# Output evictions of a second matrix product: eleven buffers of whole rows and one accumulating DMA per token tile

## The chip, the cores and the metric

The kernel runs on one core of one Trainium2 chip. The metric is the device time of one execution in microseconds (us), as the median over several runs. Differences under about half a per cent are not told apart from no change.

## What is computed

Three layers follow each other: a linear attention with a normalised output, a layer of three gates whose maximum is taken, and a mixture of four experts. Only the last is touched here:

```python
def _moe2_ref(x, domain_probs, w1, w2):
    N, D = x.shape              # 2304 tokens, 512 columns
    E = w1.shape[0]             # 4 experts, 1024 hidden columns each
    p = domain_probs / (domain_probs.sum(-1, keepdims=True) + 1e-09)
    out = np.zeros((N, D), dtype=np.float32)
    for e in range(E):
        h = np.maximum(x @ w1[e], 0.0)
        out += p[:, e:e + 1] * (h @ w2[e])
    return out.astype(np.float32)
```

## The kernel before

Every product of float32 matrices is written as three products of a rounded high part and a low rest (hi times hi, lo times hi, hi times lo), and the products of two-by-two blocks go by Strassen's scheme (in Winograd's form), with seven block products where the plain way has eight.

The layer of the experts is a sequence of 24 **visits** (`visits`, L1104). A visit is one pair (q, sb): q, from 0 to 7, is a half of an expert's hidden columns, and sb, from 0 to 2, is a super-block of 768 tokens, in two blocks (blk) of three token tiles (i) of 128 tokens. Through even q the super-blocks go 0, 1, 2, through odd q 2, 1, 0, so that two visits of three change the super-block. A visit has two halves, r = 0 and 1, and a half has seven steps k. In each step TensorE does one block product of the first matrix (`product`, L594, through `seven`, L604: 6 matmuls of 384 columns). ScalarE then brings the result out of PSUM (`after_product`, L650; the copies stand at L658), and VectorE adds it up. Between these steps stand, in portions of `AFTER = (10, 9, 9, 8, 10, 9, 8)`, the 126 matmuls (L855, 256 columns each) of the **second product of the visit before** (`second`, L842). So each visit has 84 + 126 = 210 matmuls.

The second product has seven block products j = 0 to 6, 18 matmuls each, in two parts: token tiles i = 0 and 1 (half 0), then i = 2 (half 1). When a part is done, `after_second` (L818) evicts it. For j = 0 a copy within PSUM does it (L826). For the others ScalarE (L836, j = 1, 2, 3, 6) writes an eviction buffer, scaled by the token's weight p, or VectorE (L838, j = 4, 5) adds to what stands in it. Which j belongs to which block of tokens and to which half b of the 512 output columns, in the kernel before:

| j | engine | blk, b | buffer | then sent |
|---|---|---|---|---|
| 1 | ScalarE | 1, 1 | new | no |
| 2 | ScalarE | 0, 0 | new | yes |
| 3 | ScalarE | 0, 1 | new | no |
| 4 | VectorE | 0, 1 | that of j = 3 | yes |
| 5 | VectorE | 1, 1 | that of j = 1 | yes |
| 6 | ScalarE | 1, 0 | new | yes |

There are three buffers (`new_ev`, L798), each of three pieces of 256 columns, one per token tile: one in `fa`, two in the tile `late["w2"]` (`w2s` in the profile). `put_out` (L806) sends a piece of 128 tokens x 256 columns to the output with a DMA of GpSimd's queue: as a plain store for q = 0 (L814), with addition in memory for the others (L812). Two token tiles of the eighteen are put together from two batches and need two DMAs of 64 rows each.

The order of the work is written out by hand, and each engine takes its instructions in that order. Behind the evictions on ScalarE stand the copies of L658, on which the next `product` on TensorE depends, since it writes the same PSUM bank. GpSimd also makes the sums of the weights (`w1_sums`, L530, `w2_sums`, L558). SyncE's queue loads the operands of the next super-block, 768 KB per step k, in the second half of a visit that ends with a change of super-block (`op_load`, L1118), and the weights.

Of the kernel before, what the change touches and what calls it, by code (L numbers as in the profile page):

```python
# [13 lines left out]
ALU = mybir.AluOpType  # L14
# [7 lines left out]
def tile_attn_moe_moe2(  # L22
# [23 lines left out]
    nc = tc.nc  # L46
    B, H, S, D = q.shape
    NT, DM = out.shape
    FF = w1.shape[1]
    E, _, EF = e_w1.shape  # L50
    P = 128
# [46 lines left out]
    fa = cst.tile([P, NB * KT + 2 * T], F32, name="fa")  # L98
# [4 lines left out]
    def part(t, at, n, c=None):  # L103
        ap = t[:, at : at + n]
        return ap if c is None else ap.rearrange("p (c f) -> p c f", c=c)
# [14 lines left out]
    for b0 in range(0, B, 2):  # L120
        for b, s0 in ((b0, 0), (b0, 256), (b0, None), (b0 + 1, 0), (b0 + 1, 256)):
# [3 lines left out]
            else:  # L125
                rows = out[b * S + s0 : b * S + s0 + 256, :].rearrange("(p r) d -> r p d", r=2)
# [327 lines left out]
    HK = 2 * T  # L454
# [18 lines left out]
    late = {}  # L473
# [321 lines left out]
    JACC = (0, 2, 1, 0, 2, 0, 0)  # L795
    ev_turn = [0]

    def new_ev():  # L798
        ev_turn[0] += 1
        n = ev_turn[0] % 3  # L800
        return part(fa, 12 * HK, HK) if n == 0 else late["w2"][:, (n - 1) * HK : n * HK]

    def piece(acc, i):
        return acc[i // 2][:, i % 2 * 2 * P : (i % 2 + 1) * 2 * P]

    def put_out(q, sb, blk, b, ev, i):  # L806
        t = (2 * sb + blk) * TPB + i
        n = P // len(tiles[t])
        for x, rows in enumerate(tiles[t]):
            dst, src = rows[:, b * 2 * P : (b + 1) * 2 * P], ev[x * n : (x + 1) * n, i * 2 * P : (i + 1) * 2 * P]  # L810
            if q:
                nc.gpsimd.dma_start(out=dst, in_=src, accum_op=ALU.add)  # L812
            else:
                nc.gpsimd.dma_start(out=dst, in_=src)  # L814

    held = {}

    def after_second(gi, q, sb, j, half):  # L818

        acc = [ACC[(gi + x) % 3] for x in range(3)]  # L820
        ps = acc[JACC[j]]
        e = q // 2
        its = (0, 1) if half == 0 else (2,)
        if j == 0:
            w = 4 * P if half == 0 else 2 * P
            nc.scalar.activation(out=acc[1][half][:, :w], in_=ps[half][:, :w], func=AF.Copy)  # L826
            return
        if half == 0 and j in (1, 2, 3, 6):
            held[j] = new_ev()
        ev = held[{4: 3, 5: 1}.get(j, j)]  # L830
        for i in its:
            blk = {1: 1, 2: 0, 3: 0, 4: 0, 5: 1, 6: 1}[j]
            pe = p_all[:, (2 * sb + blk) * TPB + i, e : e + 1]
            o = ev[:, i * 2 * P : (i + 1) * 2 * P]
            if j in (1, 2, 3, 6):
                nc.scalar.activation(out=o, in_=piece(ps, i), func=AF.Copy, scale=pe)  # L836
            else:
                nc.vector.scalar_tensor_tensor(out=o, in0=piece(ps, i), scalar=pe, in1=o, op0=ALU.mult, op1=ALU.add)  # L838
            if j in (2, 4, 5, 6):
                put_out(q, sb, blk, {2: 0, 4: 1, 5: 1, 6: 0}[j], ev, i)  # L840

    def second(gi, q, sb):  # L842

# [41 lines left out]
    with tc.manual_schedule():  # L885
# [75 lines left out]
        for st in steps:  # L961
            st, *en = st.split(".")
            kind = st[0]
            at = [int(st[1:])] if kind in "cds" else [int(x) for x in st[1:]]
            if kind in "cds":
                n = at[0]
# [28 lines left out]
            elif kind == "A":  # L995
                i, j, f = at
                moe1_a(i, j, f, xs[j], *en)
            elif kind == "H":
                j, f = at
# [133 lines left out]
        for q in range(1, Q):  # L1133
            e, pr, n = q // 2, q % 2 * 2, 6 * q
# [33 lines left out]
        for n in range(2 * len(visits)):  # L1168
# [10 lines left out]
            for k in range(7):  # L1179
                t = 7 * n + k  # L1180
                product(r, k)
                after_product(n, k)
                if gi == 0:
                    lag_at(7 * len(units) + t)
                    go(fill, FILL_18[1 + t])
                    if r == 0:
                        for i in SPLIT.get((0, k), ()):
                            y_split(i)
                for _ in range(AFTER[k] if gi else 0):
                    ended = next(rest, None)  # L1190
                    if ended:
                        after_second(*of, *ended)
                for step in todo.pop(t, ()):
                    step()
                if gi + 1 < len(visits):
                    turn_y(gi, r, k)
                for step in plan.pop(t, ()):
                    step()
# [5 lines left out]
        for ended in second(gi - 1, *visits[gi - 1]):  # L1204
            if ended:
                after_second(gi - 1, *visits[gi - 1], *ended)
# [33 lines left out]
```

## Time and profile before

| | |
|---|---|
| median of 3 runs | 1316.18 us (1314.63 to 1321.26) |
| profiled execution, its own time | 1327.1 us |
| span of the profile | 1325.3 us |
| busy in the span: TensorE, VectorE, ScalarE, GpSimd | 1125.6, 756.0, 599.0, 492.2 us |
| the layer of the experts in it (second products) | from 410.4 us to the end |

The profile is of one execution, 11 us above the median. Its span runs from the first instruction to the last. TensorE's matmuls overlap, so its busy time is no measure of its rate. The granted clock (1.00 is 2.4 GHz, 0.50 is 1.2 GHz) tells how fast a matmul can run.

### The profile page before, as it was taken

The numbers are of one execution on the slowest core, as the hardware profiler recorded it, in microseconds if no ns is written. First come the engines' busy times: TensorE is split into PE (matmuls) and PEld (weight loads), VectorE is DVE, ScalarE is ACT, GpSimd is POOL, SyncE is SP. The second block draws the span as 40 slices with busy tenths as digits, with TensorE's granted clock in tenths as the row PEclk, the third lists the DMA queues.
The fourth block names the chain that finished last, engine by engine and source line by source line (L and its number), as shares of the span: only waits on it lengthen the run. The fifth ranks groups of instructions, "written<-read, shape, count | busy, mean of one in ns | idle before, by whom it ended". The sixth has DMA issues, their size and how long they took to land.

```text
span 1325.3 us, 19611 instructions
## 1 busy us (share of the span) xinstructions
PE 1125.6 (85%) x7318; PEld 1097.8 (83%) x7318; DVE 756.0 (57%) x1298; ACT 599.0 (45%) x1269; POOL 492.2 (37%) x552
## 2 busy tenths in 40 slices
PE   7899999999978899797978769887877987797985
PEld 6789999999968899686978769787876987796885
DVE  3899866666677666355546435553644554455442
ACT  2542344344356555354455435454443454354443
POOL 1356434201132352344236334423533352344234
PEclk8999999999988899899989879988988988899988
DMA  9935544232176536657655685665578456758645
GB/s 247 300 100 181 191 171 134 95 126 82 60 298 221 219 111 222 197 80 207 180 106 118 154 238 80 189 151 134 82 201 242 71 114 148 212 80 211 192 56 67
DMA packets 128271, 207.63 MB, mean 157 GB/s; under 512 B 16304, under 2 KB 102832, under 8 KB 128176
## 3 DMA queue, kind: packets, MB, share of 16 engines
q1 hardware_dynamic: 88944, 168.29, 37.9%
q0 software_dynamic: 38528, 37.77, 20.8%
q8 instruction: 57, 0.93, 0.3%
q10 hardware_dynamic: 704, 0.33, 0.1%
q14 instruction: 38, 0.31, 0.1%
HBM read 136.35 MB, written 69.99 MB: 156 GB/s over the span
## 4 chain that ended last, share of the span: by engine, by line
issue 33%; POOL 18%; DMA 7%; PE 5%; ACT 1%; DVE 1%; POOLq 0%; ACTq 0%; DVEq 0%
POOL out_dram L812 12%; DMA out_dram<-w2s 4%; DMA out_dram<-fa 3%; PE bank L604 3%; POOL fa L558 3%; PE bank L855 2%; POOL w1s L530 2%; POOL out_dram L814 1%; DVE w2s L838 0%; ACT wr L633 0%; DVE wl L500 0%; ACT fa L836 0%; ACT w2s L836 0%; ACT wl L536 0%; ACT hr L633 0%
## 5 line engine op out<-in xcount | busy, mean ns | idle before, releaser
L604 PE MATMUL bank<-rb,wl 128*128 128x384 f32 x1032 | 235.3, 368 | 141.0 <-ACT bank L658 141.0
L604 PEld LDWEIGHTS bank<-rb,wl 128*128 128x128 f32 x1032 | 195.2, 209 | 148.4 <-ACT bank L658 147.1
L855 PE MATMUL bank<-wr 128*128 128x256 f32 x1683 | 273.1, 296 | 8.9 <-DVE w2s L838 8.1
L812 POOL DMA_DIRECT2D out_dram<-w2s x184 | 162.1, 1109 | 314.3 <-ACT w2s L836 155.9
L855 PEld LDWEIGHTS bank<-wr 128*128 128x128 f32 x1683 | 252.9, 204 | 11.2 <-DVE w2s L838 9.8
L658 ACT ACTIVATE fa<-bank 128x384 f32<-128x384 f32 x192 | 94.4, 492 | 211.0 <-PE bank L604 210.1
L604 PE MATMUL bank<-xr,wl 128*128 128x384 f32 x864 | 176.5, 339 | 6.2 <-DVE fa L645 4.5
L604 PEld LDWEIGHTS bank<-xr,wl 128*128 128x128 f32 x864 | 146.5, 190 | 7.5 <-DVE fa L645 5.3
L812 POOL DMA_DIRECT2D out_dram<-fa x96 | 84.5, 1101 | 167.2 <-ACT fa L836 87.3
L836 ACT ACTIVATE w2s<-bank,p_all 128x256 f32<-128x256 f32 x192 | 80.0, 475 | 134.9 <-DMA out_dram<-w2s 105.7
L530 POOL TENSOR_TENSOR w1s<-w1s 128x256 f32<-128x256 f32 x96 | 88.8, 944 | 111.5 <-DMA w1s<-w_da 48.7
L640 DVE TENSOR_TENSOR wr<-fa,wr 128x384 fp32r<-128x384 f32 x138 | 81.6, 592 | 57.2 <-ACT wr L633 57.2
L855 PE MATMUL bank<-wr,hr 128*128 128x256 f32 x567 | 94.4, 287 | 4.1 <-ACT bank L826 2.2
L855 PEld LDWEIGHTS bank<-wr,hr 128*128 128x128 f32 x567 | 83.7, 194 | 5.5 <-ACT bank L826 2.4
L633 ACT ACTIVATE wr<-fa 128x384 fp32r<-128x384 f32 x144 | 75.4, 525 | 11.3 <-DVE fa L648 6.9
L836 ACT ACTIVATE fa<-bank,p_all 128x256 f32<-128x256 f32 x96 | 40.1, 474 | 79.0 <-DMA out_dram<-fa 65.8
L638 DVE SCALAR_TENSOR_TENSOR wr<-fa,wr 128x384 fp32r<-128x384 f32 x49 | 30.1, 615 | 73.3 <-ACT wr L633 73.3
L855 PE MATMUL bank<-wr,xr 128*128 128x256 f32 x396 | 68.3, 282 | 1.5 <-DVE w2s L838 1.3
L645 DVE TENSOR_TENSOR fa<-bank,fa 128x384 f32<-128x384 f32 x96 | 53.0, 553 | 21.8 <-ACT fa L658 19.8
L604 PE MATMUL bank<-op,wl 128*128 128x384 f32 x288 | 60.4, 346 | 4.7 <-ACT fa L658 4.7
L855 PEld LDWEIGHTS bank<-wr,xr 128*128 128x128 f32 x396 | 58.5, 188 | 2.4 <-DVE w2s L838 1.9
L500 DVE TENSOR_TENSOR wl<-w1s,wl 128x768 fp32r<-128x768 f32 (+1 forms) x30 | 34.6, 1155 | 43.9 <-ACT wl L536 43.9
(196 smaller groups left out, 2011.9 us busy)
## 6 DMA issues: line engine op xcount, KB each, us to landing
rb<-op_d SPq DMA_DIRECT2D x42, 768.0 KB, 5.9
xr<-op_d SPq DMA_DIRECT2D x42, 768.0 KB, 7.6
out_dram<-w2s POOLq DMA_DIRECT2D x172, 128.0 KB, 3.9
out_dram<-fa POOLq DMA_DIRECT2D x84, 128.0 KB, 4.3
op<-op_d SPq DMA_DIRECT2D x14, 768.0 KB, 7.7
stage_a<-in_moe_w_dram SPq DMA_DIRECT2D x18, 512.0 KB, 4.0
w1s<-in_moe_w_dram SPq DMA_DIRECT2D x30, 256.0 KB, 4.5
fa<-in_moe_w_dram SPq DMA_DIRECT2D x28, 256.0 KB, 6.6
```

The lines of the kernel that those rows point to most:

```text
L500: nc.vector.tensor_tensor(out=lo, in0=src, in1=f32(hi), op=ALU.subtract)
L530: eng.tensor_tensor(out=st[o], in0=st[a], in1=st[b], op=ALU.subtract)
L558: nc.gpsimd.tensor_tensor(out=st[o], in0=st[a], in1=st[b], op=op)
L604: nc.tensor.matmul(out, w[wi][:, c * P : (c + 1) * P], y[yi][:, c, :], start=(i == 0 and k in begin), stop=(i == 5), skip_group_check=k no ...
L633: nc.scalar.activation(out=ops[key][0], in_=src, func=AF.Relu if relu else AF.Copy)
L638: nc.vector.scalar_tensor_tensor(out=lo, in0=src, scalar=0.0, in1=f32(hi), op0=ALU.max, op1=ALU.subtract)
L640: nc.vector.tensor_tensor(out=lo, in0=src, in1=f32(hi), op=ALU.subtract)
L645: todo.setdefault(t, []).append(lambda: fn(*args, **kw))
L658: nc.scalar.activation(out=out, in_=in_, func=func)
L812: nc.gpsimd.dma_start(out=dst, in_=src, accum_op=ALU.add)
L836: nc.scalar.activation(out=o, in_=piece(ps, i), func=AF.Copy, scale=pe)
L855: nc.tensor.matmul(piece(ps, i), h[hi][:, i * P : (i + 1) * P], w[wi], start=fresh, stop=last, skip_group_check=True,)
```

## The change

A buffer now holds one whole output row of 512 columns per token, for one token tile. Each visit takes six of them, three for blk 1 at j = 1 and three for blk 0 at j = 2, and all later evictions of the same tile go into the same buffer, at column 0 or 256. There are nine such places in q = 0 and eleven afterwards: four in `w2s`, four in the tile `late["ow"]` (`ob` in the profile), one in `fa`, and two more in `fa` from q = 1 on. A token tile is sent once per visit, at j = 4 (blk 0) or j = 6 (blk 1), by one DMA of 128 rows of 2 KB in place of two of 128 rows of 1 KB.

```diff
--- before.py
+++ after.py
@@ -795,23 +795,24 @@
     JACC = (0, 2, 1, 0, 2, 0, 0)
     ev_turn = [0]
 
-    def new_ev():
+    def new_ev(q):
+        fa_at = (12 * HK,) if q == 0 else (12 * HK, 16 * 2 * P, 18 * 2 * P)
+        places = [(late[x], n * DM) for n in range(4) for x in ("w2", "ow")] + [(fa, at) for at in fa_at]
         ev_turn[0] += 1
-        n = ev_turn[0] % 3
-        return part(fa, 12 * HK, HK) if n == 0 else late["w2"][:, (n - 1) * HK : n * HK]
+        return part(*places[ev_turn[0] % len(places)], DM)
 
     def piece(acc, i):
         return acc[i // 2][:, i % 2 * 2 * P : (i % 2 + 1) * 2 * P]
 
-    def put_out(q, sb, blk, b, ev, i):
+    def put_out(q, sb, blk, ev, i):
         t = (2 * sb + blk) * TPB + i
         n = P // len(tiles[t])
         for x, rows in enumerate(tiles[t]):
-            dst, src = rows[:, b * 2 * P : (b + 1) * 2 * P], ev[x * n : (x + 1) * n, i * 2 * P : (i + 1) * 2 * P]
+            src = ev[x * n : (x + 1) * n, :]
             if q:
-                nc.gpsimd.dma_start(out=dst, in_=src, accum_op=ALU.add)
+                nc.gpsimd.dma_start(out=rows, in_=src, accum_op=ALU.add)
             else:
-                nc.gpsimd.dma_start(out=dst, in_=src)
+                nc.gpsimd.dma_start(out=rows, in_=src)
 
     held = {}
 
@@ -820,24 +821,23 @@
         acc = [ACC[(gi + x) % 3] for x in range(3)]
         ps = acc[JACC[j]]
         e = q // 2
-        its = (0, 1) if half == 0 else (2,)
         if j == 0:
             w = 4 * P if half == 0 else 2 * P
             nc.scalar.activation(out=acc[1][half][:, :w], in_=ps[half][:, :w], func=AF.Copy)
             return
-        if half == 0 and j in (1, 2, 3, 6):
-            held[j] = new_ev()
-        ev = held[{4: 3, 5: 1}.get(j, j)]
-        for i in its:
-            blk = {1: 1, 2: 0, 3: 0, 4: 0, 5: 1, 6: 1}[j]
+        blk, b = {1: (1, 1), 2: (0, 0), 3: (0, 1), 4: (0, 1), 5: (1, 1), 6: (1, 0)}[j]
+        for i in (0, 1) if half == 0 else (2,):
+            if j in (1, 2):
+                held[blk, i] = new_ev(q)
+            ev = held[blk, i]
             pe = p_all[:, (2 * sb + blk) * TPB + i, e : e + 1]
-            o = ev[:, i * 2 * P : (i + 1) * 2 * P]
+            o = ev[:, b * 2 * P : (b + 1) * 2 * P]
             if j in (1, 2, 3, 6):
                 nc.scalar.activation(out=o, in_=piece(ps, i), func=AF.Copy, scale=pe)
             else:
                 nc.vector.scalar_tensor_tensor(out=o, in0=piece(ps, i), scalar=pe, in1=o, op0=ALU.mult, op1=ALU.add)
-            if j in (2, 4, 5, 6):
-                put_out(q, sb, blk, {2: 0, 4: 1, 5: 1, 6: 0}[j], ev, i)
+            if j in (4, 6):
+                put_out(q, sb, blk, ev, i)
 
     def second(gi, q, sb):
```

The order of the instructions on TensorE and SyncE is that of before. On ScalarE it is so too, with other buffers and other waits. The end of the visit that lies at 748 to 791 us in the profile stands on ScalarE as follows in the kernel before. L836 are the evictions of j = 6, the second L658 the copy on which TensorE's next product depends, and a DMASW is a wait for an output DMA:

```order
L658 ACTIVATE fa<-bank_73 128x384 [waits PE_49,Activation_49]
L633 ACTIVATE wr<-fa 128x384 [waits DVE_49]
L836 ACTIVATE w2s<-bank_66,p_all 128x256 [waits DMASW0_49,PE_49]
L836 ACTIVATE w2s<-bank_66,p_all 128x256 [waits DMASW1_49]
L836 ACTIVATE w2s<-bank_67,p_all 128x256 [waits DMASW2_49,PE_49]
L633 ACTIVATE wr<-fa 128x384 [waits DVE_49]
L658 ACTIVATE bank_72<-bank_73 128x384 [waits DVE_49,PE_49]
L633 ACTIVATE wl<-fa 128x384
L658 ACTIVATE fa<-bank_72 128x384 [waits PE_49]
```

and in the changed kernel:

```order
L658 ACTIVATE fa<-bank_73 128x384 [waits PE_49,Activation_49]
L633 ACTIVATE wr<-fa 128x384 [waits DVE_49]
L836 ACTIVATE w2s<-bank_66,p_all 128x256 [waits PE_49]
L836 ACTIVATE ob<-bank_66,p_all 128x256
L836 ACTIVATE w2s<-bank_67,p_all 128x256 [waits PE_49]
L633 ACTIVATE wr<-fa 128x384 [waits DVE_49]
L658 ACTIVATE bank_72<-bank_73 128x384 [waits DVE_49,PE_49]
L633 ACTIVATE wl<-fa 128x384
L658 ACTIVATE fa<-bank_72 128x384 [waits PE_49]
```

The evictions no longer wait for a DMA. Only the waits for TensorE are left.

GpSimd's queue at the start of q = 4 in the kernel before, behind the DMAs of j = 6: four sums for the first matrix's weights (`w1s`), the DMAs of j = 2, four sums for the second matrix's weights (in `fa`), and the first DMA of j = 4:

```order
L530 TENSOR_TENSOR w1s<-w1s 128x256 [waits DMAHW7_49,DMAHW0_49]
L530 TENSOR_TENSOR w1s<-w1s 128x256 [waits Pool_49]
L530 TENSOR_TENSOR w1s<-w1s 128x256
L530 TENSOR_TENSOR w1s<-w1s 128x256 [waits Pool_49]
L812 DMA out_dram<-w2s 128x256 [waits DMASW2_49,Activation_49]
L812 DMA out_dram<-w2s 128x256 [waits DMASW3_49,Activation_49]
L812 DMA out_dram<-w2s 128x256 [waits DMASW4_49,Activation_49]
L558 TENSOR_TENSOR fa<-fa 128x256 [waits DMAHW1_49]
L558 TENSOR_TENSOR fa<-fa 128x256 [waits DMAHW2_49,Pool_49]
L558 TENSOR_TENSOR fa<-fa 128x256
L558 TENSOR_TENSOR fa<-fa 128x256 [waits Pool_49]
L812 DMA out_dram<-w2s 128x256 [waits DMASW5_49,DVE_49]
```

and in the changed kernel, from the same sums to the first DMA of j = 4:

```order
L530 TENSOR_TENSOR w1s<-w1s 128x256 [waits DMAHW7_49,DMAHW0_49]
L530 TENSOR_TENSOR w1s<-w1s 128x256 [waits Pool_49]
L530 TENSOR_TENSOR w1s<-w1s 128x256
L530 TENSOR_TENSOR w1s<-w1s 128x256 [waits Pool_49]
L558 TENSOR_TENSOR fa<-fa 128x256 [waits DMAHW1_49]
L558 TENSOR_TENSOR fa<-fa 128x256 [waits DMAHW2_49,Pool_49]
L558 TENSOR_TENSOR fa<-fa 128x256
L558 TENSOR_TENSOR fa<-fa 128x256 [waits Pool_49]
L813 DMA out_dram<-w2s 128x512 [waits DMASW1_49,DVE_49,Activation_49]
```

The DMAs of j = 2, which wait for ScalarE, no longer stand between the two sets of sums.

## Rows read from the trace of the kernel before

**Rows 1.** Stretches (--windows): time; each engine's busy us (instructions); clock; DMA share; GB/s

```profile
core 0: us, PE busy (x) PEld busy (x) DVE busy (x) ACT busy (x) POOL busy (x), PEclk, DMA share, GB/s
674.04:707.61 33.57, 30.73 (x215) 30.33 (x214) 18.05 (x34) 17.89 (x41) 14.81 (x19) 1.00 0.45 73
825.49:868.91 43.42, 32.93 (x213) 32.32 (x212) 22.91 (x37) 20.19 (x45) 19.70 (x22) 0.90 0.68 169
868.91:910.46 41.55, 31.59 (x212) 31.18 (x211) 17.87 (x33) 16.95 (x40) 14.71 (x17) 0.91 0.73 197
910.46:945.44 34.98, 32.14 (x212) 31.73 (x211) 18.21 (x34) 17.90 (x41) 14.85 (x19) 0.94 0.44 71
512.61:1300.40 787.79, 643.13 (x4208) 633.35 (x4206) 386.86 (x696) 363.91 (x811) 314.74 (x362) 0.91 0.62 148
447.77:478.53 30.76, 30.01 (x212) 29.80 (x211) 20.69 (x36) 17.68 (x42) 13.95 (x21) 1.00 0.37 121
```

**Rows 2.** Waits from 512.61 to 1300.4 us: total us, times, longest us

```profile
PE bank L604 <- ACT bank L658: 134.6, 25, 10.3
ACT w2s L836 <- DMA out_dram<-w2s: 105.7, 41, 9.3
...
ACT fa L836 <- DMA out_dram<-fa: 54.8, 17, 8.5
```

**Rows 3.** Timeline of a visit's end: start us, us, engine line, [idle before <-releaser]

```profile
776.23 1.36 PE L855 MATMUL bank<-wr 128*128 128x256 f32 x10
780.20 0.86 POOL L812 DMA_DIRECT2D out_dram<-w2s  x1 [3.30 <-issue]
782.62 0.47 ACT L836 ACTIVATE w2s<-bank,p_all 128x256 f32<-128x256 f32 x1 [9.35 <-DMA out_dram<-w2s]
...
786.59 0.47 ACT L836 ACTIVATE w2s<-bank,p_all 128x256 f32<-128x256 f32 x1 [2.57 <-DMA out_dram<-w2s]
...
787.38 0.48 ACT L658 ACTIVATE bank<-bank 128x384 f32<-128x384 f32 x1
...
787.91 2.29 PE L604 MATMUL bank<-rb,wl 128*128 128x384 f32 x6 [10.32 <-ACT bank L658]
```

**Rows 4.** DMA queues (packets, MB, share) and output DMAs (landing us), 512.61 to 1300.4

```profile
q0 software_dynamic: 34991, 31.51, 31.5%
q1 hardware_dynamic: 32304, 84.16, 30.2%
...
out_dram<-w2s POOLq DMA_DIRECT2D x146, 128.0 KB, 4.1
```

**Rows 5.** Line L812, output DMAs: ns min/median/max on GpSimd; landing in us

```profile
L812 POOL DMA_DIRECT2D out_dram<-w2s x184: 812/906/1893, 521.7 to 1310.7; - x184
...
DMA to landing us min/median/max: 2.5/4.2/11.6
```

**Rows 6.** Line L1118, operand loads on SyncE's queue, and their landing in us

```profile
L1118 SPq DMA_DIRECT2D rb<-op_d x42: 319/319/345, 490.4 to 1243.8; - x42
...
DMA to landing us min/median/max: 4.1/7.1/8.5
```

**Rows 7.** Timeline in the middle of a visit in which q changes

```profile
837.79 1.88 DVE L500 TENSOR_TENSOR wl<-w1s,wl 128x1024 fp32r<-128x1024 f32 x1 [2.82 <-ACT wl L536]
837.86 5.39 POOL L558 TENSOR_TENSOR fa<-fa 128x256 f32<-128x256 f32 x4
...
839.59 1.07 DVE L640 TENSOR_TENSOR wr<-fa,wr 128x384 fp32r<-128x384 f32 x1
840.59 1.07 DVE L648 SCALAR_TENSOR_TENSOR fa<-fa 128x384 f32<-128x384 f32 x1
...
842.22 0.47 ACT L658 ACTIVATE bank<-bank 128x384 f32<-128x384 f32 x1 [4.05 <-DVE fa L645]
...
842.75 1.32 PE L604 MATMUL bank<-rb,wl 128*128 128x384 f32 x6 [2.83 <-ACT bank L658]
```

**Rows 8.** Timeline of VectorE in a visit without sums on GpSimd

```profile
676.00 0.55 DVE L640 TENSOR_TENSOR wr<-fa,wr 128x384 fp32r<-128x384 f32 x1
```

**Rows 9.** Timeline of the end of the program

```profile
1313.51 0.51 PE L855 MATMUL bank<-wr,hr 128*128 128x256 f32 x3
1316.03 0.47 ACT L836 ACTIVATE fa<-bank,p_all 128x256 f32<-128x256 f32 x1 [8.42 <-DMA out_dram<-fa]
...
1320.42 0.90 POOL L812 DMA_DIRECT2D out_dram<-fa  x1 [0.56 <-ACT fa L836]
```

## The prediction

> **What bounds the kernel now.** I read the stretches first. From 512.61 to 1300.40 us lie twenty visits, 787.79 us or 39.4 us each; TensorE is busy in 643.13 us of them, so 144.7 us are idle, and the mean clock is 0.91 [rows 1]. The visit from 674.04 us has clock 1.00 and 30.73 us of busy TensorE, against 31.59 us at clock 0.91 and 32.93 us at 0.90 in visits with the same 210 matmuls [rows 1]. So TensorE loses time in two ways: it stands still, and afterwards it works at a lower clock.
>
> The waits say why it stands still. Its products wait 25 times, 134.6 us in all, for ScalarE's copy L658; ScalarE's evictions L836 wait 105.7 and 54.8 us for output DMAs to leave the buffers [rows 2]. The timeline of one visit's end joins the two. TensorE's last matmuls before the gap start at 776.23 us. GpSimd issues the third DMA of j = 5 at 780.20 us. ScalarE, which must evict j = 6, waits 9.35 us for one of these DMAs, gets its first buffer at 782.62 and its third at 786.59 us; only then comes the copy at 787.38 us, and TensorE goes on at 787.91 us after 10.32 us [rows 3]. Its six matmuls then take 2.29 us, against 1.32 us for six in a visit's middle [rows 3, 7]: the low clock.
>
> The rotation of three buffers explains the place. Four new ones are taken per visit, at j = 1, 2, 3 and 6. The one for j = 6 is that of j = 1, and this is sent only at j = 5, just before. Every visit from q = 1 on ends so. Of the 25 waits, six are of another kind, in the middle of the visits in which q changes (2.83 us in [rows 7]; the six, which I added up from the timeline, are 14.4 us). The other 19 are ends of visits: 120.2 us.
>
> **The change, part by part.**
>
> *The wait at j = 6.* After the change j = 6 writes into the buffer that j = 1 took in the same visit and that nobody has sent since. The order on ScalarE shows no DMA wait there. I cost the 19 waits at their full 120 us, because a visit has nothing else that stops at this place: the two visits with clock 1.00 in [rows 1] differ by only 0.7 us of busy time, and the first of them (447.77 us, where DMAs are plain stores) has 0.75 us of idle time in its whole 30.76 us.
>
> *The low clock behind it.* The row of the same kind at clock 1.00 has 30.73 us of busy time [rows 1]. Twenty times that is 614.6 us, against 643.1: 28.5 us. The upper end comes from the 30.01 us of the visit at 447.77 us: 43 us. The lower end comes from the clock itself: 0.91 means that 18% of 787.8 us, 142 us, were at 0.50; if all 120 us of waiting lay in them, 22 us of work were left at half the rate, which loses 11 us. I take 28.5, from the nearest row.
>
> *Where the wait goes.* A buffer must still be free when it is taken again. Six are taken per visit and eleven rotate. The shortest way is from the first buffer of blk 1, sent at j = 6 of one visit, to the third of blk 0, taken at j = 2 of the next: 60 of 126 matmuls of the second product later, so 60/126 of some 31 us, 14.7 us. Output DMAs land in 4.2 us, 11.6 us at worst [rows 5]. Nothing waits there unless landing becomes longer. All other buffers have more than a visit.
>
> *DMAs of 2 KB rows.* Each visit issues 6 DMAs in place of 12 (and one more, not two, for a tile of two batches). On GpSimd that takes away some 6 times 0.91 us [rows 5] per visit, beside other work, at no gain. What a packet of 2 KB costs the DMA engines no row shows. In the stretch, queue 0 (outputs) has 34991 packets in 31.5% of 16 engines: 113 ns for packets of 0.9 KB on average; queue 1 has 32304 packets in 30.2%: 118 ns for 2.6 KB on average [rows 4]. So the cost is between one 1 KB packet (113 ns) and two (227 ns), and I take it near the former, since the larger packets of queue 1 are no dearer. Output DMAs, 12.4 us of the engines' time per visit (31.5% of 39.4), become 6 to 12 us. It lies beside TensorE's work either way; if that cover is gone, see the second rival.
> The Trainium skill, DMA: Bandwidth & Descriptors, section "Why small descriptors are slow (HBM only)", speaks against the lower end. It puts the fixed part of a packet at some 3 bus cycles, beside one cycle per 32 bytes. By that, as an estimate, a packet of 2 KB costs 67 cycles and one of 1 KB 35, so two small ones are hardly dearer than a large one and the DMA engines gain nothing. The sum would be the same 160.5 us by the rule, since the outputs are hidden either way, but the rival in which the DMA engines become the limit would deserve about twice the chance that I give it. The measured packets of queue 1 disagree with the rule, so I don't.
>
> *The middle of the visits in which q changes.* There TensorE waits 2.83 us, because VectorE is late: L640 and L648 take 1.07 us each beside GpSimd's sums L558 [rows 7], against 0.55 us without sums [rows 8]. The order on GpSimd puts these sums ahead, directly behind the sums L530, since the DMAs of j = 2 no longer stand between. VectorE's two instructions should then be 1.0 us faster. There are seven such visits (one lies before the stretch): 7 us. The upper end is the whole wait, 16 us; the lower end is nothing, as the sums then slow other instructions of VectorE.
>
> *The end.* TensorE's last group starts at 1313.51 us; ScalarE gets its first buffer for j = 6 after 8.42 us, at 1316.03 us, and the last DMA is issued at 1320.42 us [rows 9]. Without the wait the three evictions (0.47 us each) end near 1314.6 us and the third DMA is issued near 1315.5 us: 5 us, less at most 1 if landing takes longer with 256 KB.
>
> *Edits at nothing.* VectorE's additions and ScalarE's evictions are the same 128 x 256 pieces in the same order. Moving the DMAs of j = 2 to j = 4 and of j = 5 to j = 6 makes them later, but nobody but the buffers waits for them. Behind them in GpSimd's queue stand the sums, whose users come steps later.
>
> **The sum.** 120 + 28.5 + 7 + 5 = 160.5 us. Against the profiled execution that is 1327.1 - 160.5 = 1166.6 us. The profile lies 10.9 us above the median; I take the saving off the median, 1316.2 - 160.5 = **1155 us**. A visit then takes 31.4 us. The terms' ends give 135 (1181 us) and 184 us (1132 us).
>
> **The rivals.**
>
> *More comes back*: busy time falls to that of the visit at 447.77 us and the middle waits vanish. For it: the sums move to where VectorE has gaps. Against: that visit has no additions in memory beside it. 1132 us.
>
> *The DMA engines become the limit in visits that load operands.* In the visit from 868.91 us they are busy in 73% of 41.55 us, 30.3 us [rows 1]. If two packets in one save nothing, those 30.3 us must fit into 31. For it: the loads are already slow there, 7.1 us, 8.5 at worst [rows 6]. Against: an operand is issued seven steps before it is used, half a visit, 15.7 us, so landing must double to 17 us before TensorE waits; and it would then wait some 1.5 us, in 14 visits. 21 us of the gain are lost: 1176 us.
>
> *The wait moves* to the first buffer of blk 1. Landing half as long again as the worst (17.4 us) against 14.7 us, plus the eviction and the issue of some 1.4 us, makes 4 us in each of 14 visits: 56 us, 1211 us. Against it: it needs the worst landing every time.
>
> *Slower*: accumulation of 2 KB rows is so dear that the DMA queue sets the length of a visit. Queue 1 needs 30.2% of 39.4 us, 11.9 us per visit. The outputs are 48 packets per engine and visit. It is slower than now from (39.4 - 11.9)/48 = 573 ns per packet on, five times the present price. At 700 ns a visit takes 45.5 us, and twenty cost 122 us more: 1438 us. Nothing in the profile speaks for it but that accumulation of 2 KB rows is not in it.
>
> *It does nothing*: some wait of another kind keeps ScalarE at j = 6. The order leaves only TensorE's own semaphore there. 1316 us.
>
> **How the numbers follow.** Chances: forecast 0.70 (1143 to 1170 us), more comes back 0.12, the DMA engines 0.11, the wait moves 0.04, slower 0.02, nothing 0.01. Half a per cent (6.6 us) is about what can be told from no change; all cases but the last two are far beyond it: faster 0.97, same 0.01, slower 0.02. The range runs from the upper end of the terms, 1132 us, to 1190 us, past the lower end and the second rival; the third rival and what follows lie outside.
>
> **What would show it.** Right: no wait of L836 for an output DMA at j = 6; TensorE's 25 waits for L658 down to the six or seven in the middle; a clock of 0.98 or more after 512 us; visits of 30 to 33 us. Packets of queue 0 half as many, at 113 to 227 ns. Wrong: a wait of L836 or L658 with the old total at another step; TensorE waiting for operands from `op_d`; a DMA share near 1.00 through whole visits.

## The result, and the profile after

| | before, beside it | after |
|---|---|---|
| median | 1315.41 us (1314.32 to 1321.26, 4 runs) | **1151.13 us** (1149.26 to 1152.46, 4 runs) |
| ratio | | **0.874** [0.871, 0.877] |
| profiled execution, and its span | 1327.1 us, 1325.3 us | 1152.46 us, 1150.7 us |
| mean granted clock of the stretch of twenty visits | 0.91 | 1.00 |

The forecast was 1155 us. On another chip the same kernel took 1151.89 us (1151.44 to 1152.63) against 1319.8 us, a ratio of 0.873 [0.870, 0.876].

The same twenty visits now lie between 510.02 and 1127.83 us. These are the stretches of the kernel after (columns as in [rows 1]): first all twenty, then a visit in which neither the super-block nor q changes, one that loads operands while q stays, and one that loads operands while q changes.

```profile
510.02:1127.83 617.81, 602.78 (x4208) 597.06 (x4206) 388.56 (x696) 359.94 (x811) 205.01 (x229) 1.00 0.71 189
818.27:849.01 30.74, 29.99 (x212) 29.79 (x211) 18.39 (x34) 17.69 (x41) 13.98 (x16) 1.00 0.73 168
602.70:633.01 30.31, 30.05 (x212) 29.84 (x211) 17.30 (x35) 16.86 (x40) 6.12 (x7) 1.00 0.82 233
849.01:880.56 31.55, 30.31 (x212) 29.91 (x211) 22.78 (x36) 19.89 (x45) 12.58 (x14) 1.00 0.65 183
```

A visit takes 30.9 us where it took 39.4. The 787.79 us of [rows 1] are 617.81: 170.0 us less. TensorE's busy time fell by 40.4 us (643.13 to 602.78), with the same 4208 instructions, and its idle time by 129.6 us (144.7 to 15.0).

The waits of this stretch (total us, times, longest us) have no row in which L836 waits for an output DMA, and the first row of [rows 2] has become small:

```profile
ACT bank L658 <- DVE fa L645: 21.7, 10, 2.3
...
PE bank L604 <- ACT bank L658: 6.0, 6, 1.0
```

The six that are left stand in the middle of the visits in which q changes. The end of the visit of [rows 3] (now from 695.40 to 725.68 us) shows what became of the others (timeline of after: start, duration, engine and line, in brackets the idle time before and what ended it):

```profile
720.89 0.48 ACT L836 ACTIVATE w2s<-bank,p_all 128x256 f32<-128x256 f32 x1 [1.38 <-PE bank L855]
...
721.62 0.48 ACT L836 ACTIVATE w2s<-bank,p_all 128x256 f32<-128x256 f32 x1
...
722.46 1.36 PE L855 MATMUL bank<-wr 128*128 128x256 f32 x10
...
722.66 0.47 ACT L658 ACTIVATE bank<-bank 128x384 f32<-128x384 f32 x1
...
723.66 1.22 PE L604 MATMUL bank<-rb,wl 128*128 128x384 f32 x6
```

ScalarE waits only for TensorE before the first eviction of j = 6, its copy L658 is under way 1.8 us after that eviction began, and TensorE has no gap; six matmuls take 1.22 us where they took 2.29.

The middle of the visit in which q changes, beside [rows 7] (timeline of after, GpSimd, VectorE, ScalarE and TensorE):

```profile
758.44 4.10 POOL L558 TENSOR_TENSOR fa<-fa 128x256 f32<-128x256 f32 x4
...
758.82 1.08 DVE L640 TENSOR_TENSOR wr<-fa,wr 128x384 fp32r<-128x384 f32 x1
...
767.18 1.22 DVE L500 TENSOR_TENSOR wl<-w1s,wl 128x1024 fp32r<-128x1024 f32 x1 [2.43 <-ACT wl L536]
...
768.32 0.55 DVE L640 TENSOR_TENSOR wr<-fa,wr 128x384 fp32r<-128x384 f32 x1
...
769.90 0.47 ACT L658 ACTIVATE bank<-bank 128x384 f32<-128x384 f32 x1 [2.35 <-DVE fa L645]
...
770.43 1.33 PE L604 MATMUL bank<-rb,wl 128*128 128x384 f32 x6 [0.99 <-ACT bank L658]
```

GpSimd's sums are over at 762.54 us, 4.6 us ahead of VectorE's L500; in the kernel before they ran together. L500 takes 1.22 us for 1.88, the L640 behind it 0.55 for 1.07, and TensorE waits 0.99 us for 2.83. The sums now run beside earlier instructions of VectorE and slow those (the L640 at 758.82 us takes 1.08 us), but TensorE does not wait there.

The DMA queues in the stretch (packets, MB, share), for [rows 4]:

```profile
q1 hardware_dynamic: 32354, 84.37, 39.2%
q0 software_dynamic: 17557, 31.95, 31.7%
...
out_dram<-w2s POOLq DMA_DIRECT2D x40, 256.0 KB, 7.8
```

Half the packets carry the same bytes. A packet of queue 0 takes 31.7% of 617.8 us on 16 engines, divided by 17557: 178 ns, against 113. Output DMAs land more slowly than in [rows 5], and so do the operand loads of [rows 6]. The landing times of lines L813 (outputs) and L1118 (operands):

```profile
DMA to landing us min/median/max: 3.6/8.2/13.5
DMA to landing us min/median/max: 4.0/7.9/11.6
```

The end of the program, for [rows 9] (timeline of after; the span ends at 1150.70 us):

```profile
1139.43 0.52 PE L855 MATMUL bank<-wr,hr 128*128 128x256 f32 x3
...
1139.65 0.83 ACT L836 ACTIVATE fa<-bank,p_all 128x256 f32<-128x256 f32 x2
...
1142.92 0.82 POOL L813 DMA_DIRECT2D out_dram<-fa  x1 [0.92 <-issue]
1144.20 0.90 POOL L813 DMA_DIRECT2D out_dram<-fa  x1 [0.46 <-issue]
```

### The profile page after: what moved, and what is told of

Its sections match the earlier page's. It is cut to its first block, busy times and chain, and to the rows that moved or that the text cites. A ratio compares the mean times of both kernels' runs of the same rounds, so it can differ in the third digit from the quotient of the medians.

```text
span 1150.7 us, 19292 instructions
## 1 busy us (share of the span) xinstructions
PE 1083.1 (94%) x7318; PEld 1059.4 (92%) x7318; DVE 759.9 (66%) x1298; ACT 595.2 (52%) x1269; POOL 364.8 (32%) x392
## 4 chain that ended last, share of the span: by engine, by line
PE 49%; DVE 5%; issue 4%; ACT 3%; POOL 1%; POOLq 0%; ACTq 0%; DVEq 0%
PE bank L604 25%; PE bank L855 24%; DVE wl L500 1%; ACT wl L536 1%; DVE ob L838 1%; DVE fa L648 1%; POOL out_dram L813 1%; DVE w2s L838 1%; ACT wr L633 1%; DVE fa L838 1%; ACT fa L836 0%; ACT bank L658 0%; ACT ob L836 0%; DVE fa L645 0%; DVE wr L640 0%
## 5 line engine op out<-in xcount | busy, mean ns | idle before, releaser
L855 PE MATMUL bank<-wr 128*128 128x256 f32 x1683 | 258.5, 284 | 8.9 <-DVE w2s L838 5.1
L855 PEld LDWEIGHTS bank<-wr 128*128 128x128 f32 x1683 | 236.5, 191 | 11.2 <-DVE w2s L838 5.5
L604 PE MATMUL bank<-rb,wl 128*128 128x384 f32 x1032 | 212.0, 341 | 10.6 <-ACT bank L658 10.5
L658 ACT ACTIVATE fa<-bank 128x384 f32<-128x384 f32 x192 | 94.7, 493 | 188.6 <-PE bank L604 181.9
L604 PEld LDWEIGHTS bank<-rb,wl 128*128 128x128 f32 x1032 | 176.6, 189 | 14.1 <-ACT bank L658 12.8
L604 PE MATMUL bank<-xr,wl 128*128 128x384 f32 x864 | 176.4, 339 | 5.9 <-DVE fa L645 4.3
L604 PEld LDWEIGHTS bank<-xr,wl 128*128 128x128 f32 x864 | 146.4, 190 | 7.2 <-DVE fa L645 5.0
L530 POOL TENSOR_TENSOR w1s<-w1s 128x256 f32<-128x256 f32 x96 | 86.8, 924 | 153.3 <-DMA w1s<-in_moe_w_dram 90.5
L640 DVE TENSOR_TENSOR wr<-fa,wr 128x384 fp32r<-128x384 f32 x138 | 83.2, 603 | 56.6 <-ACT wr L633 56.6
L813 POOL DMA_DIRECT2D out_dram<-w2s x49 | 52.3, 1093 | 147.3 <-DVE ob L838 88.5
L813 POOL DMA_DIRECT2D out_dram<-ob x50 | 52.4, 1085 | 128.9 <-DVE fa L838 27.8
L813 POOL DMA_DIRECT2D out_dram<-fa x41 | 39.1, 1085 | 106.3 <-DVE fa L838 26.7
L836 ACT ACTIVATE ob<-bank,p_all 128x256 f32<-128x256 f32 x106 | 50.4, 475 | 30.9 <-PE bank L855 30.9
L645 DVE TENSOR_TENSOR fa<-bank,fa 128x384 f32<-128x384 f32 x96 | 52.9, 551 | 19.6 <-ACT fa L658 17.5
L604 PE MATMUL bank<-op,wl 128*128 128x384 f32 x288 | 60.5, 346 | 5.0 <-ACT fa L658 5.0
L747 DVE TENSOR_TENSOR fa<-bank,fa 128x384 f32<-128x384 f32 x54 | 29.9, 554 | 51.3 <-ACT fa L744 36.0
L836 ACT ACTIVATE w2s<-bank,p_all 128x256 f32<-128x256 f32 x106 | 50.4, 476 | 22.3 <-PE bank L855 22.3
```

What stands on the lines that cost most here:

```text
L530: eng.tensor_tensor(out=st[o], in0=st[a], in1=st[b], op=ALU.subtract)
L604: nc.tensor.matmul(out, w[wi][:, c * P : (c + 1) * P], y[yi][:, c, :], start=(i == 0 and k in begin), stop=(i == 5), skip_group_check=k no ...
L640: nc.vector.tensor_tensor(out=lo, in0=src, in1=f32(hi), op=ALU.subtract)
L645: todo.setdefault(t, []).append(lambda: fn(*args, **kw))
L658: nc.scalar.activation(out=out, in_=in_, func=func)
L747: nc.vector.tensor_tensor(out=mx[done] if i == 0 else t, in0=x, in1=t, op=ALU.add)
```

## The experiments

Each ran beside the kernel before on its own chip; ratios are to that. Where a line tells of "the theory", it is that of the prediction: the buffers were the bound, not the DMAs.

### One more buffer, and nothing else

```diff
-        n = ev_turn[0] % 3
-        return part(fa, 12 * HK, HK) if n == 0 else late["w2"][:, (n - 1) * HK : n * HK]
+        n = ev_turn[0] % 4
+        return part(fa, 12 * HK, HK) if n == 0 else late["ow"][:, :HK] if n == 3 else late["w2"][:, (n - 1) * HK : n * HK]
```

> The kernel before with a fourth eviction buffer of three pieces of 256 columns (768 of the columns of ob), nothing else: still twelve DMAs of 1 KB rows per visit. Theory (the gain is the wait at j = 6 for the buffer sent at j = 5, and the low clock behind it): with four in rotation each of j = 1, 2, 3, 6 has its own buffer, sent a visit earlier; no DMA wait at j = 6, visits of 30 to 33 us, clock 0.99 or more from 512 us on. The DMAs of j = 2 still stand between the sums on GpSimd, so the waits in the middle of the q-changing visits stay 2.0 to 2.8 us: 1151 + 7 x 1.2 = 1160 us (1152 to 1172). Rival (the gain is that of fewer and larger DMAs): at least 1250 us, with waits of ScalarE for output DMAs left.

Measured: 1167.02 us (1164.50 to 1170.64) against 1318.62, a ratio of 0.884 [0.881, 0.888]. A fourth buffer, with all DMAs of 1 KB rows where they were, brings 152 us, where the rival (the gain is that of larger DMAs) allowed at most 70. Its twenty visits as one stretch, and their waits:

```profile
505.91:1139.88 633.97, 607.79 (x4208) 600.59 (x4206) 389.42 (x696) 360.94 (x811) 320.42 (x362) 0.99 0.77 184
```
```profile
PE bank L604 <- ACT bank L658: 14.3, 6, 2.7
ACT w2s L836 <- DMA out_dram<-w2s: 9.9, 8, 1.8
PE bank L604 <- ACT fa L658: 2.9, 6, 0.9
```

The 19 waits at the ends of visits are gone, and with them 35.3 us of TensorE's busy time (643.13 to 607.79). The eight waits of L836 that are left are short and stand at j = 1. The six waits in the middle have stayed: 14.3 us, as before. What causes them stands in its timeline, VectorE and GpSimd side by side (the last experiment tests this):

```profile
768.35 1.89 DVE L500 TENSOR_TENSOR wl<-w1s,wl 128x1024 fp32r<-128x1024 f32 x1 [2.17 <-ACT wl L536]
768.42 5.40 POOL L558 TENSOR_TENSOR fa<-fa 128x256 f32<-128x256 f32 x4
770.16 1.07 DVE L640 TENSOR_TENSOR wr<-fa,wr 128x384 fp32r<-128x384 f32 x1
...
773.32 1.70 PE L604 MATMUL bank<-rb,wl 128*128 128x384 f32 x5 [2.71 <-ACT bank L658]
```

### The change, with each row sent in two halves

```diff
-            src = ev[x * n : (x + 1) * n, :]
-            ...
-                nc.gpsimd.dma_start(out=rows, in_=src, accum_op=ALU.add)
+            for b in range(2):
+                cols = slice(b * 2 * P, (b + 1) * 2 * P)
+                dst, src = rows[:, cols], ev[x * n : (x + 1) * n, cols]
+                ...
+                    nc.gpsimd.dma_start(out=dst, in_=src, accum_op=ALU.add)
```

> The changed kernel, but each token tile is sent as two DMAs of 1 KB rows, one per column half, at the same places (j = 4 and 6). Theory: the buffers still come free in time, 1151 us (1147 to 1160); 113 ns per packet, so 227 ns per row where the changed kernel shows 177, and the DMA share in visits that load operands rises from 0.82 to about 0.90. Rival (the size of the DMAs carries the gain): 1180 us or more.

Measured: 1171.27 us (1169.18 to 1174.49), ratio 0.887 [0.884, 0.891]: 20 us more than the change, where I expected at most 9 more. The DMA engines are not the reason. Their packets cost what I had expected (115 ns for 1 KB, by the queue's row for the twenty visits: 39.3% of 634.0 us on 16 engines, divided by 34813):

```profile
q0 software_dynamic: 34813, 31.82, 39.3%
```

The stretches show first a visit that loads operands, with the largest DMA share of all kernels here, 0.94, and still 30.32 us; the extra time lies in visits like the second, in which q changes:

```profile
602.65:632.97 30.32, 30.05 (x212) 29.86 (x211) 17.32 (x35) 16.86 (x41) 12.85 (x15) 1.00 0.94 235
950.18:985.12 34.94, 31.94 (x212) 31.33 (x211) 22.92 (x36) 20.11 (x44) 18.82 (x21) 0.95 0.76 189
```

The six visits of that kind are 13.8 us longer than in the change, of 16.2 us for all twenty; the end of the program is 2.3 us longer (25.21 us for 22.87). GpSimd issues twelve DMAs per visit again, and its sums come late. The timeline of the second of the two visits shown:

```profile
955.87 2.03 DVE L500 TENSOR_TENSOR wl<-w1s,wl 128x768 fp32r<-128x768 f32 x1 [2.38 <-ACT wl L536]
956.00 4.51 POOL L530 TENSOR_TENSOR w1s<-w1s 128x256 f32<-128x256 f32 x4
...
957.82 1.09 DVE L645 TENSOR_TENSOR fa<-fa 128x384 f32<-128x384 f32 x1
...
958.84 0.54 DVE L645 TENSOR_TENSOR fa<-bank,fa 128x384 f32<-128x384 f32 x1
...
960.47 4.24 POOL L558 TENSOR_TENSOR fa<-fa 128x256 f32<-128x256 f32 x4
...
961.64 1.47 DVE L500 TENSOR_TENSOR wl<-w1s,wl 128x1024 fp32r<-128x1024 f32 x1 [1.73 <-ACT wl L536]
963.03 1.09 DVE L640 TENSOR_TENSOR wr<-fa,wr 128x384 fp32r<-128x384 f32 x1
...
966.21 2.29 PE L604 MATMUL bank<-rb,wl 128*128 128x384 f32 x6 [2.25 <-ACT bank L658]
```

Both sets of sums run beside VectorE: L530 beside the first part of the split, and L558 beside the second part and the L640 behind it, which take 1.47 and 1.09 us for the 1.22 and 0.55 of the change. The wait of 2.25 us is back, and the six matmuls behind it take 2.29 us. So the merged DMAs are worth 20 us here, and the most of it by GpSimd's time and order and not by the DMA engines'. My expectation had overlooked that the sums stand behind the DMAs in GpSimd's queue. That is read from the timeline: no run has halved rows and the sums out of VectorE's way.

### The change, with six places in place of eleven

```diff
-        return part(*places[ev_turn[0] % len(places)], DM)
+        return part(*places[ev_turn[0] % 6], DM)
```

> The changed kernel with six places in rotation in place of nine and eleven: the first buffers of blk 1, sent at j = 6, are taken again at j = 1 of the next visit, 36 of 126 matmuls later, 8.8 us. Eviction, issue and a landing of 8.2 us (the changed kernel's median) need 9.6 us. Theory (what counts is the time from sending to taking again): ScalarE waits for output DMAs at j = 1, 1 to 5 us in most visits, TensorE is partly covered: 1165 to 1230 us. Rival (fewer, larger DMAs carry the gain, the number of buffers matters little): 1151 us, within 5.

Measured: 1220.30 us (1213.76 to 1223.66), ratio 0.924 [0.919, 0.928]. The wait of L836 comes back, at another step, and with it TensorE's wait for L658. It stands at j = 1, where the first buffers of blk 1 are taken again (waits of the first nineteen of the twenty visits):

```profile
ACT ob L836 <- DMA out_dram<-ob: 45.3, 23, 3.7
PE bank L604 <- ACT fa L658: 40.4, 13, 4.6
ACT w2s L836 <- DMA out_dram<-w2s: 14.1, 12, 1.8
PE bank L604 <- ACT bank L658: 6.0, 6, 1.0
```

### The change, with nine places

```diff
-        return part(*places[ev_turn[0] % len(places)], DM)
+        return part(*places[ev_turn[0] % 9], DM)
```

> The changed kernel with nine places in rotation throughout (without the two further ones in fa). The buffer taken again soonest is then the first of blk 1, 54 of 126 matmuls after it is sent, 13.2 us at 30.9 us per visit; eviction, issue and landing need 9.6 us with the median landing of 8.2, 14.9 us with the longest of 13.5. Theory (only the time from sending to taking again counts, and six places gave 8.8 us): no or a few waits of ScalarE under 2 us, 1150 to 1156 us. Rival (six places cost 68 us by their number, nine should cost some 25 of it): 1165 us or more.

Measured: 1152.57 us (1151.47 to 1156.00) against 1323.0, ratio 0.872 [0.869, 0.876]. Its trace has three waits of L836 for a DMA, 1.9 us in all. Between sending and taking again lie 36 of the 126 matmuls with six places, 54 with nine and 60 with eleven: 8.8, 13.2 and 14.7 us. Landing takes 8.2 us in the median and 13.5 at worst (L813 of the kernel after). So six are too few, nine just suffice, and eleven add nothing that can be measured.

### The kernel before, with idle matmuls in the gap at the end of a visit

```diff
+                if gi >= 4 and (r, k) == (1, 6) and gi + 1 < len(visits) and visits[gi][1] != visits[gi + 1][1]:
+                    for _ in range(32):
+                        nc.tensor.matmul(
+                            ACC[gi % 3][0][:, :P], ident, ident, start=True, stop=True, skip_group_check=True
+                        )
```

> The kernel before with 32 matmuls of 128 x 128 x 128 on a constant (some 7 us, into a PSUM bank that is free then; their result is not used) at the end of each visit with a change of super-block from the fifth on, where TensorE waits 7 to 10 us. The wait itself stays. Theory (the 40 us more of TensorE's busy time in the kernel before come from the low clock behind the waits): the clock stays higher, the work behind the wait runs at 1.00, 1.5 to 2.5 us less in each of 13 visits, 1280 to 1300 us. Rival (the busy time is longer for another reason, such as late operands): no change beyond 5 us, or slower by the matmuls added.

Measured: 1304.01 us (1301.54 to 1309.93), ratio 0.987 [0.983, 0.991]. 95.0 us of added work on TensorE make the kernel 14.6 us shorter; I had expected 19 to 39. A visit that loads operands, and of it the added matmuls alone (stretch as in [rows 1], the second row only with PE and PEld; each of the 32 matmuls counts as two instructions):

```profile
749.21:788.73 39.52, 37.43 (x277) 37.02 (x276) 18.24 (x35) 16.97 (x40) 13.89 (x16) 1.00 0.77 208
749.21:788.73 39.52, 7.31 (x64) 7.23 (x64) 1.00 0.77 208
```

Without the 7.31 us, its own work takes 30.1 us at clock 1.00, where a visit of the same kind in the kernel before takes 31.59 at 0.91 [rows 1]. So the low clock is a cost of its own behind the waits. In the two profiles TensorE's own work takes 620.5 us in the twenty visits where it took 643.13, 22.6 us less, while the added matmuls and what is left of the idle time take 150.6 us where 144.7 were idle (all twenty visits, and of them the added matmuls alone):

```profile
511.87:1283.01 771.14, 715.51 (x5040) 706.47 (x5038) 388.80 (x696) 363.44 (x812) 316.13 (x362) 0.98 0.64 151
511.87:1283.01 771.14, 94.98 (x832) 93.99 (x832) 0.98 0.64 151
```

The size fell short of what I had expected since some waits remain behind the added matmuls: 1.83 us in this visit, up to 3.4 us in others, and some visits still show a clock of 0.93 to 0.96.

### The change, with plain stores

```diff
-                nc.gpsimd.dma_start(out=rows, in_=src, accum_op=ALU.add)
+                nc.gpsimd.dma_start(out=rows, in_=src)
```

> The changed kernel with plain stores in place of additions in memory for q from 1 on (the output keeps one visit's share per row, not the sum). Theory (TensorE sets the pace, the DMAs are covered): the same time within 4 us, less at most 2 us at the end, where the last DMA lands earlier; packets of queue 0 under 177 ns. Rival (the DMA engines set the length of the visits that load operands): at least 8 us less.

Measured: 1147.39 us (1145.28 to 1149.50, two runs), ratio 0.870 [0.866, 0.874], 4.5 us below the change on the same chip. I had allowed 4 us, at most 2 of them at the end. The twenty visits take 617.62 us, against 617.81: no difference. In the profiles of that chip 3.8 us are gained at the end, where the last stretch takes 18.59 us in place of 22.37, and 2.8 us ahead of the twenty visits, where nothing was changed. Yet the DMA engines' work differs much (the queue in the twenty visits, and the landing of L813):

```profile
q0 software_dynamic: 10042, 32.23, 13.2%
```
```profile
DMA to landing us min/median/max: 2.3/6.1/8.9
```

The addition costs the DMA engines 2.4 times the time of a plain store (31.7% against 13.2%) for the same bytes, which go in 17557 packets with the addition and in 10042 larger ones without. All of this time lies beside TensorE's work except at the program's end.

### The change, with the split of the weights one step later

L500 and its copy L536 stand at step 5 of the first half of a visit, ahead of the work that TensorE waits for. Here they stand at step 6.

```diff
-            at(n, 5, w1_split, 1, 1)
+            at(n, 6, w1_split, 1, 1)
```

> The changed kernel with the second split of the first matrix's weights one step later (k = 6 in place of 5 of the half before its use), so that VectorE's long subtraction L500 stands behind the addition L645 for which the copy L658 waits. Theory (what is left of the wait in the middle of the q-changing visits, 0.99 us in each of seven, comes from L500 ahead of L645): these waits vanish, 7 us less than the changed kernel on the same chip (4 to 9). Rival (the split is then late for product 2 of the next half, or the time is lost elsewhere): no change within 2 us, or slower.

Measured: **1141.57 us** (1140.87 to 1143.85, 5 runs), ratio 0.866 [0.863, 0.868], against 1151.89 us for the change on the same chip: 10.3 us less, where I had expected 4 to 9. It beats both kernels. All twenty visits, and one in which q changes:

```profile
508.06:1118.41 610.35, 601.38 (x4208) 596.90 (x4206) 388.30 (x696) 359.94 (x811) 206.24 (x229) 1.00 0.73 192
...
843.60:873.91 30.31, 30.06 (x212) 29.86 (x211) 23.18 (x38) 19.89 (x45) 11.57 (x13) 1.00 0.67 189
```

No wait of TensorE for L658 is left in its twenty visits, and the visits in which q changes (31.55 us in the change) are as short as the others. Each of the seven is some 1.3 us shorter, 9.1 us in all in the two profiles, where the wait itself was 0.99.

### Both small edits, and no rows of 2 KB

The fourth buffer of the first experiment, and the split one step later.

```diff
-        n = ev_turn[0] % 3
+        n = ev_turn[0] % 4
...
-            at(n, 5, w1_split, 1, 1)
+            at(n, 6, w1_split, 1, 1)
```

> The kernel before with a fourth buffer (as the first experiment) and the split of the weights one step later. Theory (the 14 us by which the first experiment stays behind the changed kernel are the waits of 2.0 to 2.7 us in the middle of the q-changing visits, with the lower clock behind some of them, because the sums on GpSimd run beside L500): these waits fall below 1 us, 1150 to 1158 us. Rival (the 14 us come from the twice as many small DMAs themselves): 1160 to 1167 us.

Measured: 1149.70 us (1147.12 to 1151.50), ratio 0.871 [0.869, 0.874]. Against the fourth buffer alone (on the other chip) that is 17 us less: the wait in the middle, with the low clock behind it, is worth that much. With four buffers and DMAs of 1 KB rows, the time of the whole change is reached; the rows of 2 KB and the eleven places together bring 8 us more (1141.57) once the split stands later. No run separates these two: with four buffers L836 still waits seven times for an output DMA, 8.4 us in all, and TensorE 2.1 us for an L658 behind it.

## Why the prediction was right

The time came out 4 us below the forecast, and by the steps that the prediction gave; that it came so close is partly luck, as the last paragraph of this section shows. Term by term, by the two profiles (spans 1325.3 and 1150.7 us, 174.6 us apart):

| term | forecast | measured | from |
|---|---|---|---|
| the wait at j = 6 | 120 us | 121 us | what is left of 129.6 us less idle time, without the 8.4 us below |
| the low clock behind it | 28.5 us (11 to 43) | 40.4 us, the middle waits' share with it | busy time 643.13 to 602.78 us |
| visits in which q changes | 7 us (0 to 16) | 8.4 us, and 2.2 in the one before the stretch | six waits, 14.4 to 6.0 us |
| the end | 5 us | 2.0 us | 24.90 to 22.87 us |
| sum | 160.5 us | 174 us | |

**The wait at j = 6** was removed whole and came back nowhere. One more buffer alone shows it to be the cause, six places show that it returns where the time between sending and taking again is too short, and nine that eleven are more than is needed.

**The low clock** was sized too small. The step that failed is the choice of the visit at 674.04 us as the measure of an undisturbed one. Visits without the wait have 29.96 to 30.36 us of busy time, nearer to the 30.01 us of the visit at 447.77 us, which I had kept as the upper end. The visit at 674.04 us was no undisturbed one: it has a wait of 2.08 us at its end, and its row counts 215 instructions of TensorE where most others have 212 (timeline of before):

```profile
705.51 1.31 PE L604 MATMUL bank<-rb,wl 128*128 128x384 f32 x6 [2.08 <-ACT bank L658]
```

The fourth buffer alone gave back 35.3 of the 40.4 us, so at least this much stood behind the waits at j = 6. The added matmuls show the mechanism from the other side.

**The visits in which q changes** went as argued: the sums move away from the instructions of VectorE that TensorE waits for, and L640 falls from 1.07 to 0.55 us. I had named only L640 and L648; L500 gains 0.7 us as well. That the sums then slow other instructions of VectorE, my lower end, happened too, at a place where nobody waits. The Trainium skill, SBUF — State Buffer, section "Who interferes with whom", says that a VectorE instruction with two inputs in SBUF contends with a GpSimd instruction that reads SBUF, and one with at most one such input (outside modes that use the second port) does not. The two L645 in the trace of the halved rows agree: beside GpSimd's L530, the one that reads `fa` twice took 1.09 us and the one that reads `bank` and `fa` 0.54.

**The end** gave 2 us and not 5. The evictions came early, as I said, but my sum had room for one issue behind the last eviction. GpSimd has four to make (one token tile needs two), of 0.82 to 1.15 us each, against evictions 0.4 us apart, and with pauses of 0.92 and 0.46 us that no row explains. The last one lands 5.6 us after its issue, where the last one of before took 4.0. I had allowed 1 us for that.

**The packet of 2 KB** was bounded by 113 and 227 ns, and taken near the former. It took 178 ns, about midway; it cost nothing, since the DMA engines' work lies beside TensorE's either way. The choice compared unlike packets: those of queue 0 were accumulated, those of queue 1 were not. With plain stores a packet of queue 0 took 130 ns (13.2% of 617.6 us on 16 engines, divided by 10042) for 3.2 KB on average. By the rule of the Trainium skill, DMA: Bandwidth & Descriptors, section "Why small descriptors are slow (HBM only)", I had estimated 67 cycles to 35, 1.91 times the price of 1 KB. Measured is 178 to 113, or 1.57 times: between the rule and my choice.

**The rivals.** The DMA engines did not become the limit: visits that load operands take 30.3 us at a DMA share of 0.82, and as much at 0.94 with halved rows. Their operand loads did slow down, to 11.6 us at worst, but the half visit between issue and use is 15. The wait did not move, as it does with six places. "More comes back" had the right clock term, but not the whole middle wait. The 31.4 us that I gave for a visit took the end and the seventh visit off the twenty as well; by the terms alone it is 31.7, and it became 30.9.

By the medians the saving is 164.3 us and not 174.6: the profiled execution of before was 11.7 us longer than its median, that of after 1.3. The terms were sized in that longer execution and came out 14 us short there, most of it in the low clock; taking them off the shorter median made up for 10 of the 14 us. That is luck and no better sizing. In which of the terms those 10 us lie is open.

## What to carry to other kernels

Where an eviction buffer goes out by DMA, count the time between its sending and its next use in the worst case, and compare it with the landing under load: 8.8 us against a landing of up to 13.5 cost 69 us here, 13.2 us cost nothing. A stall of TensorE costs more than its length, because the work behind it runs at a lower clock (0.91 in the stretch before, 1.00 after): 120 us of waits took 35 us or more with them. And a cheaper order on a side engine counts: fewer DMA issues in front of GpSimd's sums, or VectorE's long instruction one step later, were worth 10 to 20 us, while sending the outputs with less than half the DMA engines' time was worth nothing in the visits.

## What the runs showed of the hardware

- Accumulating DMAs of the same bytes kept the DMA engines busy 2.4 times as long as plain ones, in 1.7 times as many packets, and landed in 8.2 us in the median in place of 6.1.
- A DMA share of 0.94 through a whole visit did not slow TensorE (30.32 us).
- Behind waits of the same length the clock is not always the same. With halved rows, five visits of the same kind have waits of 2.24 (twice), 2.25, 2.26 and 2.27 us in the middle; the six matmuls of L604 behind them took 1.33 (twice), 2.29, 1.32 and 2.29 us. What decides this is open.
